# Expert tiles run among the chunks of the recurrence, in an order worked out ahead

## Chip, core and metric

One core of a Trainium2 chip runs the whole program. The metric is the device time of one execution in microseconds. Engines are named as the profile does: PE is TensorE, DVE VectorE, ACT ScalarE, POOL GpSimd, SP the queue that issues plain DMAs.

## What is computed

A gated recurrence over 4 sequences of 5056 tokens with 256 features, and then a layer of 8 experts of which each of the 20224 tokens uses the one with the largest cosine score:

```python
sig = 1.0 / (1.0 + np.exp(-f_logit))
f = lower_bound + (1.0 - lower_bound) * sig
h = f[:, t] * h + (1.0 - f[:, t]) * x[:, t]      # for each t; y[:, t] = h
...
logits = (y / norm(y)) @ (emb / norm(emb)).T / tau
expert_idx = np.argmax(logits, axis=1)
gate_w = softmax(logits) at expert_idx
out[mask] = gate_w[mask, None] * (np.maximum(y[mask] @ w1[e], 0.0) @ w2[e])   # for each expert e
```

w1 is 256 x 1024 and w2 is 1024 x 256 for each expert.

## The kernel before

Every instruction is recorded as an operation with its engine and what it depends on (`Prog.op`). Each engine executes its operations in the order in which they were recorded; `resolve` turns the dependences into semaphore waits. So the program's text sets the order on each of the five queues.

The recurrence goes over 40 chunks of 512 tokens (the last has 256). For a chunk, `load` brings 512 tokens of f_logit and x through SP into one of three input buffers each; `F_` and `X_` turn them on PE, eight f32 transposes each, into two PSUM banks each; `gate_` makes the gate (ACT); `scan_` forms nx and runs the scan of both feature halves (DVE); `yo_` turns the result back, `yev_` copies it to the row buffer `Yt` (ACT), `sq_` squares it (ACT). Two chunks form a group for the router (the last two chunks are groups of their own, 21 groups in all): `lg_` makes logits and squared norms (PE), `rt_` turns them, `d1_` finds the expert, `psl_` counts with small matmuls the place of each token in its expert's rows of a scratch tensor in device memory (XsScratch), `d2_` and `d3_` finish place and weight, and one indirect DMA per 128 tokens on POOL scatters rows of 264 bf16 (256 features, weight, token number) there. The loop over `c` records these stages some chunks apart, and every second chunk one of the 16 weight loads (`wload`, POOL, f32 to bf16).

After the last group the number of tokens per expert is known. Some 20 small DVE instructions make the list of tiles (`tbl`: first row and expert of each of 86 tiles of 256 rows), 16 indirect DMAs fill the rows behind each expert's last token with null rows (L904), and the expert tiles follow: `xload` brings a tile through SP at an address read from the list, `yt_` turns it (four bf16 transposes, DVE copy), `mm1` does 16 w1 matmuls into four banks, ACT and DVE apply the relu, `mm2` does 16 w2 matmuls into two banks, ACT and DVE apply the weight, and two indirect DMAs on POOL write the 256 rows of the output (L1019). Each tile load waits for all scatters:

```python
scat_all = [scat[g] for g in range(NG)]
a_done = [h_tr, h_te, scat_all, h_nt]
...
xsh[j] = op(
    "sp", fn, a_done, hnull if j >= NFULL else None,
    odh[j - NX] if j >= NX else None, dma=f"xs{j % NX}",
)
```

There are six tile buffers (`NX`), two of the turned tile, two of the hidden layer, four of the output (`NO`). The four banks of `mm1`, the two of `mm2` and the two of `yt_` are the eight that the recurrence used.

Of the kernel before, what the change touches and what calls it, by code (L numbers as in the profile page):

```python
# [2 lines left out]

# [3 lines left out]
P = 128  # L7
# [8 lines left out]
class Handle:  # L16
    __slots__ = ("eng", "fn", "deps", "dma", "val", "know", "used")

    def __init__(self, eng, fn, deps, dma):
        self.eng, self.fn, self.deps, self.dma = eng, fn, deps, dma  # L20
        self.val, self.know, self.used = 0, None, False


class Prog:

    def __init__(self):
        self.order = []
        self.dma_count = {}  # L30

    def op(self, eng, fn, *deps, dma=None):
        flat = []

        def add(d):
            if d is None:
                return
            if isinstance(d, (list, tuple)):
                for x in d:
                    add(x)  # L40
            else:
                flat.append(d)

        add(deps)
        h = Handle(eng, fn, flat, dma)
        if dma is not None:
            self.dma_count[dma] = self.dma_count.get(dma, 0) + 16
            h.val = self.dma_count[dma]
        self.order.append(h)
        return h  # L50

    def resolve(self):
        for h in self.order:
            for d in h.deps:
                d.used = True
        count, know, plan = {}, {}, {}
        for h in self.order:
            kn = know.setdefault(h.eng, {})
            waits = {}
            for d in h.deps:  # L60
                key = d.dma if d.dma is not None else d.eng
                if kn.get(key, 0) >= d.val:
                    continue
                waits[key] = max(waits.get(key, 0), d.val)
            for d in h.deps:
# [6 lines left out]
            if h.dma is None and h.used:  # L72
                count[h.eng] = count.get(h.eng, 0) + 1
                h.val = count[h.eng]
            h.know = dict(kn)
            plan.setdefault(h.eng, []).append((h, sorted(waits.items())))
        return plan

    def emit(self, nc, es, block):
# [3 lines left out]
        def sem(key):  # L83
            if key not in sems:
                sems[key] = es.enter_context(nc.semaphore(name=f"s_{key}"))
            return sems[key]

        for eng, items in plan.items():
            for h, waits in items:
                for key, _ in waits:  # L90
                    sem(key)
                if h.dma is not None:
                    sem(h.dma)
                elif h.used:
                    sem(eng)

        def run(eng):
            def body(e):
                for h, waits in plan.get(eng, []):
                    for key, v in waits:  # L100
                        e.wait_ge(sems[key], v)
                    with nc.allow_low_precision(reason="whole numbers below 2**24"):
                        ins = h.fn(e)
                    if h.dma is not None:
                        ins.then_inc(sems[h.dma], 16)
                    elif h.used:
# [11 lines left out]
def bass_hgrn_recurrence__then__cosine_router_kernel(  # L118
# [23 lines left out]
    NFULL = (N - E * (T - 1) + T - 1) // T  # L142
    NT = N // T + E - 1
    NULLROW = E * CAP
    MAGIC = 12582912.0

# [7 lines left out]
    with ExitStack() as es:  # L154
# [6 lines left out]

        ident = sb("ident", [P, P])
# [6 lines left out]
        half = sb("half", [P, 8])  # L169
        scr = sb("scr", [P, P])  # L170
        iop = sb("iop", [P, 1])
        io17 = sb("io17", [P, 17])
        ex17 = sb("ex17", [P, 17])
        base17 = sb("base17", [P, 17])
        nio = sb("nio", [P, E, 2])
# [7 lines left out]
        w1b = sb("w1b", [P, E, DT, Fdim], BF16)  # L183
        w2b = sb("w2b", [P, E, FT, D], BF16)

        xin = [sb(f"xin{q}", [P, 4, D]) for q in range(3)]
        fin = [sb(f"fin{q}", [P, 4, D]) for q in range(3)]
        th = [sb(f"th{q}", [P, DT, CH]) for q in range(2)]
        fg = [sb(f"fg{q}", [P, DT, CH]) for q in range(2)]
        nx = [sb(f"nx{q}", [P, DT, CH]) for q in range(2)]  # L190
        hb = [sb(f"hb{q}", [P, DT, CH]) for q in range(4)]
        sq = [sb(f"sq{q}", [P, DT, CH]) for q in range(3)]
        lgS = [sb(f"lgS{q}", [P, CH]) for q in range(2)]
        NY = 4
# [887 lines left out]
```

## Time and profile before

| | |
|---|---|
| median of 3 runs | 820.59 us (818.81 to 821.49) |
| the profiled execution | 821.09 us, span 819.3 us |
| mean granted TensorE clock | 0.856 of full speed |
| busy in the span: PE, DVE, ACT, POOL | 606.0, 390.4, 332.6, 414.0 us |

The busy times are sums over the span; which engine matters differs by stretch. Granted clock 1.00 is 2.4 GHz, 0.5 is 1.2 GHz; a mean between them says how much of a stretch ran at each.

### The profile page before, as it was taken

What the parts mean: (1) busy time and instruction counts of PE and PEld (TensorE: products, weight loads), DVE (VectorE), ACT (ScalarE), POOL (GpSimd) and SP (SyncE); (2) the same over time, 40 slices, a digit from 0 to 9 for tenths busy, and PEclk for the clock granted to TensorE, in tenths of its full rate; (3) what the DMA queues carried; (4) which work ended last, traced back from release to release, by engine and by line L of the source; (5) the groups of instructions that cost most, each with busy time, mean ns of one, the idle gap of its engine ahead of it and who ended that gap; (6) DMA issues with size and microseconds to landing.
All of it is one profiled execution on the core that took longest, in us unless ns stands there. A gap on an engine that the chain in (4) does not pass through costs nothing.

```text
span 819.3 us, 14640 instructions
## 1 busy us (share of the span) xinstructions
PE 606.0 (74%) x4649; PEld 456.7 (56%) x4649; DVE 390.4 (48%) x817; ACT 332.6 (41%) x503; POOL 414.0 (51%) x466
## 2 busy tenths in 40 slices
PE   3665666665666665656033999999999999999994
PEld 3444455444445444442012777777777777777773
DVE  3555555555444444454121555555555555555552
ACT  4644444445454445452000433333433343344331
POOL 4056655555565564553773444444444444444443
PEclk9977777778777877785555999999999999999998
DMA  9756566766656664400121223333322332323220
GB/s 262 232 154 157 155 155 171 159 163 183 163 175 155 171 159 127 122 26 14 50 69 44 86 86 99 98 99 95 96 93 93 99 99 93 97 89 96 80 61 13
DMA packets 78868, 95.02 MB, mean 116 GB/s; under 512 B 9217, under 2 KB 68877, under 8 KB 78800
## 3 DMA queue, kind: packets, MB, share of 16 engines
q1 hardware_dynamic: 54416, 53.06, 22.3%
q0 software_dynamic: 24384, 41.02, 18.2%
q8 instruction: 46, 0.75, 0.4%
q14 instruction: 22, 0.18, 0.1%
HBM read 69.83 MB, written 34.44 MB: 127 GB/s over the span
## 4 chain that ended last, share of the span: by engine, by line
PE 70%; issue 10%; ACT 7%; DVE 6%; POOL 3%; another core or an unknown queue 2%; DMA 1%; SPq 0%; POOLq 0%; DVEq 0%; ACTq 0%
PE y_ps L994 18%; PE fl_ps L965 12%; PE xT_ps L965 11%; PE xT_ps L492 7%; PE fl_ps L477 6%; PE y_ps L558 6%; PE lg_ps L584 5%; ACT sq L548 3%; ACT Yt L571 3%; POOL XsScratch L777 2%; DVE nx L520 2%; PE lg_ps L940 1%; PE rt_ps L940 1%; PE rt_ps L631 1%
## 5 line engine op out<-in xcount | busy, mean ns | idle before, releaser
L1019 POOL DMA_INDIRECT out_dram<-osb,xsb x172 | 169.5, 986 | 202.6 <-ACT hT L980 152.2
L777 POOL DMA_INDIRECT XsScratch<-Yt,sli x158 | 155.1, 981 | 144.5 <-DVE Yt L759 100.1
L994 PE MATMUL y_ps<-w2b,hT 128*128 x1376 | 165.3, 274 | 0.9 <-DVE osb L1012 0.9
L994 PEld LDWEIGHTS y_ps<-w2b,hT 128*128 128x128 bf16 x1376 | 131.4, 98 | 15.4 <-issue 1.1
L965 PE MATMUL fl_ps<-ys,w1b 128*128 128x256 bf16 x688 | 104.1, 284 | 17.1 <-DVE ys L950 14.9
L571 ACT ACTIVATE Yt<-y_ps 128x1024 bf16<-128x1024 f32 (+1 forms) x40 | 40.5, 1013 | 181.6 <-PE y_ps L558 168.7
L1009 ACT ACTIVATE osb<-y_ps,xsb 128x256 f32<-128x256 f32 x86 | 40.8, 474 | 177.6 <-PE y_ps L994 175.7
L965 PE MATMUL xT_ps<-ys,w1b 128*128 128x256 bf16 x688 | 103.6, 283 | 0.2 <-issue 0.2
L965 PEld LDWEIGHTS fl_ps<-ys,w1b 128*128 x688 | 66.3, 96 | 60.8 <-issue 40.6
L584 PE MATMUL lg_ps<-hb,eT 128*8 128x512 f32 (+1 forms) x160 | 54.8, 784 | 57.6 <-ACT sq L548 57.6
L538 DVE TENSOR_TENSOR_SCAN hb<-fg,hb,nx 128x512 f32<-128x512 f32 (+4 forms) x78 | 93.5, 1238 | 1.4
L985 DVE TENSOR_SCALAR hT<-fl_ps 128x512 bf16<-128x512 f32 x86 | 59.5, 692 | 59.6 <-PE fl_ps L965 56.6
L1012 DVE TENSOR_SCALAR osb<-y_ps,xsb 128x256 f32<-128x256 f32 x86 | 41.6, 484 | 91.1 <-PE y_ps L994 90.1
L644 DVE TENSOR_REDUCE rmax<-rt_ps 128x8 f32<-128x64 f32 (+2 forms) x21 | 4.6, 221 | 167.1 <-issue 92.5
L492 PE MATMUL xT_ps<-ident,xin 128*128 128x128 f32 x316 | 67.0, 381 | 22.8 <-DVE nx L520 16.3
L492 PEld LDWEIGHTS xT_ps<-ident,xin 128*128 128x128 f32 x316 | 53.8, 200 | 50.7 <-issue 32.1
L965 PEld LDWEIGHTS xT_ps<-ys,w1b 128*128 x688 | 66.5, 97 | 25.2 <-issue 1.6
L985 DVE TENSOR_SCALAR hT<-xT_ps 128x512 bf16<-128x512 f32 x86 | 59.5, 692 | 42.8 <-PE xT_ps L965 30.9
L980 ACT ACTIVATE hT<-xT_ps 128x512 bf16<-128x512 f32 x86 | 51.4, 597 | 44.0 <-PE xT_ps L965 38.4
L980 ACT ACTIVATE hT<-fl_ps 128x512 bf16<-128x512 f32 x86 | 51.3, 596 | 28.9 <-PE fl_ps L965 13.3
L510 ACT ACTIVATE fg<-th,cs 128x512 f32<-128x512 f32 (+1 forms) x80 | 60.3, 801 | 1.3
L477 PE MATMUL fl_ps<-ident,fin 128*128 128x128 f32 x316 | 58.5, 347 | 1.1 <-ACT th L504 1.1
(123 smaller groups left out, 685.7 us busy)
## 6 DMA issues: line engine op xcount, KB each, us to landing
fin<-in_f_logit_dram SPq DMA_DIRECT2D x39, 512.0 KB
xin<-in_x_dram SPq DMA_DIRECT2D x39, 512.0 KB
xsb<-XsScratch SPq DMA_DIRECT2D x86, 132.0 KB
w1b<-in_moe_w_dram POOLq DMA_DIRECT2D x8, 512.0 KB, 5.9
w2b<-in_moe_w_dram POOLq DMA_DIRECT2D x8, 512.0 KB, 12.2
out_dram<-osb,xsb POOLq DMA_INDIRECT x172
XsScratch<-Yt,sli POOLq DMA_INDIRECT x158
fin<-in_f_logit_dram SPq DMA_DIRECT2D x1, 256.0 KB
```

The source lines that it names most:

```text
L477: i = e.transpose(fl_ps[:, dh, b * P : (b + 1) * P], fin[q][:, b, dh * P : (dh + 1) * P], ident[:],)
L492: i = e.transpose(xT_ps[:, dh, b * P : (b + 1) * P], xin[q][:, b, dh * P : (dh + 1) * P], ident[:],)
L510: lambda e, dh=dh: e.activation(fg[q][:, dh, 0:n], th[q][:, dh, 0:n], AF.Identity, bias=cs[:, dh, 0:1], scale=cs[:, dh, 1:2],),
L538: lambda e, dh=dh, s0=s0, s1=s1, init=init: e.tensor_tensor_scan(hb[c % 4][:, dh, s0:s1], fg[q][:, dh, s0:s1], nx[q][:, dh, s0:s1], init, ...
L571: lambda e: e.activation(Yt[g % NY][:, k_ * 4 : k_ * 4 + nb, 0:D], y_ps[:, 0:nb, :], AF.Copy),
L584: i = e.matmul(lg_ps[32 * k_ : 32 * k_ + 8, 0:n], eT[:, kt, :], hb[c % 4][:, kt, 0:n], start=(kt == 0), stop=(kt == DT - 1),)
L777: lambda e, j=j, b=b, k_=k_: e.indirect_dma_start(out=Xs[:, :], out_offset=bass.IndirectOffsetOnAxis(ap=sli[g % 4][:, j : j + 1], axis=0), ...
L965: i = e.matmul(ph[g][:, fi * T : (fi + 1) * T], w1b[:, bass.ds(ev, 1), kt, f * P : (f + 1) * P], ys[j % 2][:, kt, :], start=(kt == 0), sto ...
L980: lambda e, g=g, o=o: e.activation(o, ph[g], AF.Relu),
L985: lambda e, g=g, o=o: e.tensor_scalar(o, ph[g], 0.0, None, op0=ALU.max),
L994: i = e.matmul(po[s], hT[j % 2][:, kf, s * P : (s + 1) * P], w2b[:, bass.ds(ev, 1), kf, :], start=(kf == 0), stop=(kf == FT - 1),)
L1019: lambda e, s=s: e.indirect_dma_start(out=out[:, :], out_offset=bass.IndirectOffsetOnAxis(ap=xsb[j % NX][:].bitcast(I32)[:, s, 129:130], a ...
```

## The change

The instructions are no longer executed in the order of the text. Each operation now names what it reads, writes and which PSUM bank it uses, an estimated cost and a priority (`pr.prio`); dependences follow from the names. `schedule` then walks through the program as a small model of five engines and one DMA bus would: at each step the engine that is free first takes the ready operation with the smallest priority. The order that comes out is the order on each queue.

The list of tiles is made in eight steps (`update_`): after groups 5, 7, 9, 11, 13, 15 and 17 the tiles that are certain to be full by then are appended, 17 after the first and 8 after each of the next six, and the last 21 after group 20. A tile depends on the scatters up to its step's group, and only the last 21 wait for the null rows, which eight plain DMAs on SP now write in place of 16 indirect ones on POOL. All tiles still wait for all 16 weight loads; these are recorded one per chunk (chunks 0 to 15). A chunk's operations have the chunk's number as priority; the tiles of a step that follows chunk k have k + 3, k + 3.5, k + 4 and so on.

The first 70 tiles use three banks: 5 for the transposes and two of the four w1 pieces, 6 for the other two, 7 for w2. The recurrence keeps banks 0 to 4: `F_`, `X_` and `Y_` now work in halves of a chunk with one bank each, four transposes and one eviction at a time. The router's gate (`gate_`) is done for two groups at once, so scatters come in batches of 16, and the scaling of the norms moves from POOL to DVE. The list holds the expert's offset in the weights ready for use in place of its number.

```diff
+        for k in x:
+            edge(self.writer.get(("x", k)), True)
+            self.writer[("x", k)] = o
...
+    def schedule(self):
...
+        bus = 0.0
+        out = []
+        while True:
+            best = None
+            for e in free:
+                while wait[e] and wait[e][0][0] <= free[e]:
...
+                break
+            s, e = best
+            if avail[e]:
+                p, i, o = heapq.heappop(avail[e])
...
+                t, p, i, o = heapq.heappop(wait[e])
+            o.start = s
+            free[e] = s + o.cost
+            if o.dma is not None:
+                bus = max(bus, free[e]) + o.nbytes / self.DMA_RATE
+                o.end = max(bus, free[e]) + self.DMA_FIX
+            else:
...
+            out.append(o)
+            for q, hard in succ[id(o)]:
+                t = (o.end + self.LAT) if hard else free[e]
+                if q.eng == e and o.dma is None and hard:
+                    t = o.end + 60
+                ready[id(q)] = max(ready[id(q)], t)
+                left[id(q)] -= 1
+                if left[id(q)] == 0:
...
+        def wload(i, c):
...
+            op(
+                "pool", lambda e: e.dma_start(dst, src), 1000, w=[("w", i)], dma=f"w{i}",
+                r=[("hb", c % NH, 0)], nbytes=1 << 20,
+            )
+
...
+        batches = [[g, g + 1] for g in range(0, NG - 3, 2)] + [[g] for g in range(NG - 3, NG)]
+        bof = {g: (i, bb.index(g)) for i, bb in enumerate(batches) for g in bb}
...
         def F_(c):
...
+            for dh in range(DT):
+                def fn(e, dh=dh):
...
+
...
+                pe(fn, 135 * nb, r=[("fin", q), "ident"], x=[BF])
...
+                )
...
         def X_(c):
...
+
+                pe(fn, 135 * nb, r=[("xin", q), "ident"], x=[BX])
...
-            for dh in range(DT):
+                    n, r=[("fg", c % 2, dh)], w=[("nx", c % 2, dh)], x=[BX],
...
+        def Y_(c):
...
+            pe(
+                lg, 3000, x=[BL],
+                r=["eT", "onesf"] + [("hb", c % NH, d) for c in cc for d in range(2)]
+                + [("sq", c % NSQ) for c in cc],
+            )
...
+        def gate_(bi):
...
+            pool(
+                lambda e: e.tensor_tensor(nr2[q][:, 0:JJ], nrm[q][:, 0:JJ], half[:, 0:JJ], ALU.pow),
+                1900, r=[("nrm", q), "half"], w=[("nr2", q)],
+            )
+            dve(
+                lambda e: e.tensor_scalar(
+                    nr2[q][:, 0:JJ], nr2[q][:, 0:JJ], 1e-6, tau, op0=ALU.add, op1=ALU.mult
+                ),
+                8, r=[("nr2", q)], w=[("nr2", q)],
+            )
...
+                        op(
...
+                            1280, r=[("Yt", y), ("Ytg", y), ("Yti", y), ("ytz", y), ("sli", y)],
+                            w=[("Xs", g)], dma=f"sc{y}", nbytes=67584, chain=False,
+                        )
...
+        def update_(u, g, last):
...
+            pe(
+                lambda e: e.matmul(
+                    bank[BT][:, 456:464], onesb[:], fin_oh[:, 64:72], start=True, stop=True
+                ),
+                100, r=[("oh", (g + 1) % 3), "onesb"], x=[BT],
+            )
...
+            dve(
+                lambda e: e.tensor_tensor(acc[b][:], acc[a][:], dac[:], ALU.add),
+                2, r=["dac0", "dac1", ("acc", a)], w=[("acc", b)],
+            )
+            dve(
+                lambda e: e.tensor_scalar(
+                    tbl[u][:, 0:1], acc[b][:, 0:1], iop[:, 0:1], float(T),
+                    op0=ALU.add, op1=ALU.mult,
+                ),
+                1, r=[("acc", b), "iop"], w=[("tbl", u)],
+            )
+            dve(
+                lambda e: e.tensor_copy(tbl[u][:, 1:2], acc[b][:, 1:2]), 1,
+                r=[("acc", b)], w=[("tbl", u)],
+            )
+            if last:
+                for e_ in range(E):
+                    def nul(e, e_=e_):
...
+                    op(
+                        "sp", nul, 700, r=["nrow", "nulr"], w=["nul"], dma="nu", nbytes=135168,
+                        chain=False,
...
+        def tile_(j, u, g, phb, pob, ysb):
...
+            rd = [("tbl", u), ("nt", 0), ("nt", 1)]
+            rd += [("Xs", g_) for g_ in range(g + 1)]
+            if last:
+                rd += ["nul"]
+            op("sp", ld, 700, r=rd, w=[("xsb", qx)], dma=f"xs{qx}", nbytes=135168)
+
+            ysT = bank[ysb][:, 0:256].bitcast(BF16)
...
+            pr.prio -= YBOOST
+            pe(yt, 310, r=[("xsb", qx), "identb"], x=[ysb])
+            dve(
+                lambda e: e.tensor_copy(ys[qy][:].rearrange("p k c -> p (k c)"), ysT),
+                512, True, x=[ysb], w=[("ys", qy)],
+            )
...
+            for m in range(4):
+                pb = phb[m % len(phb)]
+
+                def mm1(e, m=m, pb=pb):
+                    if m == 0:
+                        evr[j] = e.value_load(
+                            tbl[u][j : j + 1, 1:2], min_val=0, max_val=(E - 1) * WE
+                        )
...
+                                wb[0][:, bass.ds(evr[j] + (kt * Fdim + (2 * m + fi) * P), P)],
...
+                prev = pe(
+                    mm1, 490, r=[("ys", qy), ("tbl", u)] + [("w", i) for i in range(2 * E)],
+                    x=[pb], order=[prev],
+                )
...
+            po = [bank[pob[0]][:, 0:D], bank[pob[1]][:, D : 2 * D]]
+            one = pob[0] == pob[1]
+            for m in range(4):
+                def mm2(e, m=m):
...
+                                wb[1][:, bass.ds(evr[j] + kf * D, D)],
...
+                pe(
+                    mm2, 480, r=[("hT", qh, m)] + [("w", i) for i in range(2 * E)],
+                    x=sorted(set(pob)), order=[prev],
+                )
...
+                    1280, r=[("osb", qo, s), ("xsb", qx)], w=[("out", j, s)], dma=f"od{qo}_{s}",
+                    nbytes=131072,
...
+        last_of = {cc[-1]: g for g, cc in enumerate(groups)}
+        ups = [5, 7, 9, 11, 13, 15, 17] + [NG - 1]
+        avail = []
+        for u, g in enumerate(ups):
+            tok = sum(nof(c) for gg in range(g + 1) for c in groups[gg])
+            k = max(0, -(-(tok - E * (T - 1)) // T)) if u < len(ups) - 1 else NT
+            avail += [(u, g)] * (k - len(avail))
+        MERGED = 70
+        NWC = 16
+        YBOOST = 1.5
+
+        def put(j):
+            u, g = avail[j]
+            pr.prio = groups[g][-1] + 3.0 + 0.5 * (j - avail.index((u, g)))
+            if j < MERGED:
+                tile_(j, u, g, (5, 6), (7, 7), 5)
+            else:
+                tile_(j, u, g, (0, 1, 2, 6), (3, 7), 4)
+
+        for c in range(NCH):
+            pr.prio = c
+            if c >= 2:
+                load(c)
+            F_(c)
+            X_(c)
+            Y_(c)
+            for i in range(2 * E * c // NWC, 2 * E * (c + 1) // NWC):
+                if i < 2 * E:
+                    wload(i, c)
...
+            if c in last_of:
+                g = last_of[c]
+                route_(g)
+                bi, gi = bof[g]
+                if g == batches[bi][-1]:
+                    gate_(bi)
+                if g in ups:
+                    u = ups.index(g)
+                    update_(u, g, g == NG - 1)
+        for j in range(NT):
+            put(j)
+        pr.prio = 1 << 20
+        op("pool", lambda e: e.nop(), 50, deps=[pr.writer[("out", j, s)] for j in range(NT) for s in range(2)],
...
+        pr.total = pr.schedule()
```

## Rows read from the trace of the kernel before

**Rows 1.** Busy us by engine (x count) in stretches of the span, clock, DMA

```profile
core 0: us, PE busy (x) PEld busy (x) DVE busy (x) ACT busy (x) POOL busy (x), PEclk, DMA share, GB/s
100.00:300.00 200.00, 124.62 (x812) 95.11 (x816) 105.11 (x226) 96.99 (x124) 118.76 (x124) 0.76 0.63 163
300.00:340.00 40.00, 24.08 (x152) 17.66 (x144) 19.12 (x40) 18.23 (x24) 19.74 (x22) 0.74 0.51 144
391.00:444.00 53.00, 8.00 (x49) 4.31 (x49) 8.19 (x47) 3.03 (x7) 35.89 (x42) 0.54 0.20 60
444.00:809.00 365.00, 361.37 (x3072) 278.16 (x3072) 186.81 (x340) 140.36 (x256) 166.97 (x170) 0.99 0.28 88
```

**Rows 2.** Chain that ended last, low clock: start us, us, what

```profile
158.34 1.97 PE xT_ps L492 x8
160.31 1.71 PE fl_ps L477 x8
...
181.82 1.72 PE y_ps L558 x8
...
216.19 1.97 PE xT_ps L492 x8
```

**Rows 3.** The same chain at full clock, with a group's router work

```profile
185.58 0.60 PE lg_ps L584
...
187.48 1.03 PE xT_ps L492 x8
188.51 0.87 PE fl_ps L477 x8
...
193.25 0.56 PE rt_ps L631 x4
...
195.16 0.24 PE rt_ps L697
...
195.73 1.13 issue
...
209.23 0.89 PE y_ps L558 x8
```

**Rows 4.** Groups of instructions: busy us, mean ns | idle before, releaser

```profile
L777 POOL DMA_INDIRECT XsScratch<-Yt,sli x158 | 155.1, 981 | 144.5 <-DVE Yt L759 100.1 <-issue 41.8 <-DVE q L848 1.1
L685 POOL TENSOR_SCALAR nr<-nr 128x8 f32<-128x8 f32 (+2 forms) x21 | 15.2, 725 | 1.9
L456 POOL DMA_DIRECT2D w2b<-in_moe_w_dram x8 | 8.0, 995 | 0.4
L730 DVE RECIPROCAL rs<-nr 128x8 f32<-128x8 f32 (+2 forms) x21 | 4.1, 193 | 19.0 <-POOL nr L685 18.9
```

**Rows 5.** Timeline of one expert tile: start us, us, engine, line

```profile
604.51 0.60 ACT L980 ACTIVATE hT<-xT_ps 128x512 bf16<-128x512 f32 x1 [0.43 <-PE xT_ps L965]
...
604.81 0.39 PE L940 MATMUL rt_ps<-identb,xsb 128*128 128x128 bf16 x4
605.03 1.91 PE L994 MATMUL y_ps<-w2b,hT 128*128 x16
...
605.62 0.41 DVE L950 COPY ys<-rt_ps 128x512 bf16<-128x512 bf16 x1
...
607.08 1.15 PE L965 MATMUL fl_ps<-ys,w1b 128*128 128x256 bf16 x8
608.15 1.15 PE L965 MATMUL xT_ps<-ys,w1b 128*128 128x256 bf16 x8
```

**Rows 6.** DMA issues: count, KB each, us from issue to landing

```profile
w2b<-in_moe_w_dram POOLq DMA_DIRECT2D x8, 512.0 KB, 12.2
```

**Rows 7.** PE's timeline: first, last of the recurrence, first tile

```profile
11.00 1.97 PE L477 MATMUL fl_ps<-ident,fin 128*128 128x128 f32 x8
...
391.18 0.64 PE L558 MATMUL y_ps<-ident,hb 128*128 128x128 f32 x4
...
424.90 0.58 PE L940 MATMUL lg_ps<-identb,xsb 128*128 128x128 bf16 x4 [9.78 <-DMA xsb<-XsScratch]
```

More of the change, by code (lines that the diff above doesn't have):

```diff
@@ L13 @@
 AX = mybir.AxisListType
[L16 to L21, printed above, removed]
+class Op:
+    __slots__ = (
+        "eng", "fn", "deps", "order", "dma", "val", "know", "used", "cost", "nbytes", "prio",
+        "idx", "start", "end", "tag",
+    )
 class Prog:
+    LAT = 90
+    DMA_FIX = 1900
+    DMA_RATE = 300.0
@@ L28, in __init__, with op, edge @@
     def __init__(self):
[L29 to L36, printed above, removed]
+        self.ops = []
+        self.writer = {}
+        self.readers = {}
+        self.dma_last = {}
+        self.prio = 0
+    def op(self, eng, fn, cost, r=(), w=(), x=(), deps=(), order=(), dma=None, nbytes=0, prio=None, tag="", chain=True):
+        o = Op()
+        o.eng, o.fn, o.cost, o.dma, o.nbytes = eng, fn, cost, dma, nbytes
+        o.val, o.know, o.used, o.tag = 0, None, False, tag
+        o.prio = self.prio if prio is None else prio
+        o.idx = len(self.ops)
+        need, order = {}, {id(q): q for q in order if q is not None}
+        def edge(q, bank=False):
+            if q is None or q is o:
@@ L37, in add @@
                 return
[L38 to L50 removed]
+            if (
+                q.eng == eng and q.dma is None and dma is None and (eng == "pe" or bank)
+            ):
+                order[id(q)] = q
+            else:
+                need[id(q)] = q
@@ new lines, in flat @@
+        def flat(t):
+            if t is None:
+                return
+            if isinstance(t, (list, tuple)):
+                for y in t:
+                    yield from flat(y)
+            else:
+                yield t
+        for q in flat(deps):
+            need[id(q)] = q
+        for k in r:
+            edge(self.writer.get(k))
+            self.readers.setdefault(k, []).append(o)
+        for k in w:
+            if chain:
+                edge(self.writer.get(k))
+            for q in self.readers.get(k, ()):
+                edge(q)
+            self.writer[k] = o
+            self.readers[k] = []
@@ L71, in resolve @@
                         kn[k] = v
[L72 to L76, printed above, removed]
+            o.know = dict(kn)
+            plan.setdefault(o.eng, []).append((o, sorted(waits.items())))
         return plan
```

1250 lines of the change are left out of this document (583 added, 667 removed).

## Prediction

> **What bounds the kernel now.** I read four views, in this order. First the busy time by stretch [rows 1]. It shows a kernel in three pieces. From 11 us to about 391 us the recurrence and the router run, and in the 200 us sampled there no engine is full: TensorE (PE) 62%, VectorE (DVE) 53%, ScalarE (ACT) 48%, GpSimd (POOL) 59%, at a mean granted clock of 0.76. From 391 to 444 us nearly nothing runs on PE (8.0 us busy in 53). From 444 to 809 us the expert tiles keep PE busy for 361 of 365 us at clock 0.99, while DVE and ACT are busy 51% and 38%. So the first piece is bound by waits between engines whose queues are in order, the second by the last scatters, the tile list and the first loads, the third by PE. Second, the chain of waits in the first piece: the same transposes stand there at both clock levels [rows 2, 3], 1.97, 1.71 and 1.72 us for eight at 1.2 GHz and 1.03, 0.87 and 0.89 at 2.4 GHz. The start of the same step six chunks apart gives the pace: (216.19 - 158.34)/6 = 9.64 us a chunk [rows 2]. Third, the instruction groups [rows 4]: POOL issues 330 indirect DMAs at 0.98 us, plus 0.30 us of issue time between two (41.8 us over 137 gaps), so 1.28 us each. Fourth, PE's timeline in the third piece [rows 5]: the transposes of a tile, its 16 w2 matmuls and 16 w1 matmuls follow without holes; 365/86 = 4.24 us a tile.
>
> **What PE has to do in all.** At 2.4 GHz a chunk costs PE 1.03 + 0.87 + 0.89 for its three transposes, and half a group's router work: logits 187.48 - 185.58 = 1.90, transposes 0.56, prefix matmuls 195.73 - 195.16 = 0.57 [rows 3]. That is 2.79 + 1.52 = 4.30 us, or 170 us for 39.5 chunks. The 86 tiles take 365 us. Together 535 us, against a span of 819.3: 11.0 us of lead-in [rows 7], some 210 us in which the first piece waits or is clocked low, 53 us of hole, 10.3 us of tail (819.3 - 809) [rows 1]. The change can take from the 210 and the 53; it takes no matmul away.
>
> **Part by part.**
> (a) *Weights.* One load per chunk instead of one per two, for chunks 0 to 15; each tile still waits for all 16. The last is issued after the scan of chunk 15 and lands some 12.2 us later [rows 6]. So no expert matmul can start before 16 chunks are through, however early the list is there.
> (b) *Pace until then.* With half a load per chunk the DMA engines are busy 0.63 x 9.64 = 6.1 us a chunk, without 0.51 x 9.64 = 4.9 [rows 1]; with a whole one about 7.3. POOL: 118.8 us in 20.75 chunks is 5.7, plus some 1.4 of issue gaps; half a load more (1.0 + 0.3)/2 = 0.65, the scaling of the norms moved to DVE -0.7/2 = -0.35 [rows 1, 4]: 7.4. PE needs 4.3 to about twice that by its clock, DVE and ACT 5. The halved evictions (tanh, copy to Yt, nx) add instructions on engines that are half idle. So the pace lies between 7.4 and today's 9.64. I take 8.0, nearer to the queue bounds, because four transposes and a half eviction in place of eight and a whole one halve each step that the next engine waits for. 16 x 8.0 = 128 us, and 12 us for the weights, in which PE does 1.5 chunks more.
> (c) *Merged stage.* 22 chunks are left. Priorities are chunk number against 14, 14.5, ... for the tiles; up to the last chunk 59 tiles come before it (17 + 5 x 8 + 2), that is 2.7 per chunk. PE's work: 22 x 4.30 + 59 x 4.24 = 95 + 250 = 345 us, or 15.7 us per chunk. POOL per chunk: 6.1 without weight loads + 2.7 x 2 x 1.28 = 13.0 (83%). DVE: 105.1/20.75 = 5.1, + 2.7 x 186.8/86 = 5.9, + the updates, about 17 small instructions at 0.19 us [rows 4] per four chunks, 0.8: 11.8 (75%). ACT 4.7 + 4.4 (58%). So PE stays the fullest, but POOL is close, and its scatters come in batches of 16 (20.5 us) between which the tiles' output must pass. How much of the stage PE loses to waits no row shows: the third piece loses 1%, the first 38% [rows 1]. With two independent streams to take work from I place it near the former: 12%, 345/0.88 = 392 us; the ends are 349 and 556.
> (d) *PSUM.* The merged tile has banks 5, 6 and 7 only. Bank 5 takes the transposes, two w1 pieces and three evictions: 0.39 + 0.41 + 2 x (0.53 + 0.60) [rows 5], about 3.1 us plus six handovers, under the 5.8 us (15.7/2.7) between tiles. Nothing added.
> (e) *Address arithmetic.* Each w1 matmul still takes one register step, now on a ready product. Today eight take 608.15 - 607.08 = 1.07 us, 134 ns each; the w2 ones, one step per two, about 1.91/16 = 119 [rows 5]. A gain is at most 15 ns x 1376 = 21 us; a loss of the same size isn't excluded. I take 0.
> (f) *End of the recurrence.* The last list waits for the route of chunk 39, its scatters and eight null writes, moved to SP (on POOL they are 16, 16 x 1.28 = 20 us; eight at that price would be 10 us beside the scatters). Today 424.90 - 391.18 = 34 us pass from the last transposes to the first tile [rows 7]. Six tiles (25 us) are left to cover about 30. I take 5 us, between 0 and 17. If nothing were left as cover it would cost 30. All loads of the last 21 tiles queue behind the null writes on SP; chunk loads are through by then.
> (g) *Queues.* SP is passed by 65 tile loads that used to follow the last chunk load. A tile load waits for a free buffer, hence for the output scatter six tiles earlier, and a chunk load behind it waits too. Three input buffers hide two to three chunks of that, 31 to 47 us at 15.7; I cost it at nothing, and rival C prices it.
> (h) *Rest.* 27 tiles at 4.24 = 114 us, tail 10.3.
>
> **Sum**: 11 + 128 + 12 + 392 + 5 + 114 + 10 = 672 us of span; the profiled execution took 821.1 at a span of 819.3, so 674, on a base whose median is 820.6.
>
> **A rule weighed.** The granted clock was 0.99 while PE was 99% busy and 0.76 while it was 62% busy [rows 1]. The Trainium skill, TensorE: Matmul & The Clock Gate, section "A second HAM failure mode: psum-queue depth-cycling", says that matmul groups that cycle through PSUM banks can idle so often for short times that the clock swings between its levels. It speaks against the three banks of (d). No row of this kernel shows it, as the third piece has eight banks in use; rival B is what it would do.
>
> **Rivals.**
> A, *late start*: the weights or the first lists come late behind scatters on POOL, and tiles begin some eight chunks later; the change then does half of what it says. Each such chunk leaves PE 8.0 - 4.30 = 3.7 us idle: +30, 704 us. For it: every tile waits for all weights, and the DMA engines run close to full; against: POOL has slack.
> B, *clock*: the merged stage runs at the 0.76 of the first piece. 345/0.76 = 454 us instead of 392: 736. For it: PE pieces there stay half a microsecond long between waits; against: two streams fill it.
> C, *slower*: the queues lock. Chunk loads stand behind tile loads on SP, these behind output scatters, these behind batches of 16 scatters on POOL, and PE keeps the 62% of today's first piece: 345/0.62 = 556, in all 838. It decides from the point where the merged stage exceeds 392 + 147 = 539 us, a PE share of 64%.
> D, *better*: the first 16 chunks at 7.4 (118 us), 5% lost in the merged stage (363), no hole at the end: 630.
>
> **How the numbers follow.** Forecast 674 with 0.60, A 0.13, B 0.13, C 0.06, D 0.08. The bounds of the unknown costs move the sum by -44 (D) to about +75 (9.64 a chunk is +26, 20% lost instead of 12% is +39, the hole 17 instead of 5 is +12), so I give 625 to 755, which leaves out C, half of D and the far end of B. A measurement here tells 0.3% from no change. Faster 0.93, same 0.01, slower 0.06, all of the last from C.
>
> **What would show it.** Right: first expert matmul at about 150 us; from there to some 540 us both kinds of work in every slice, PE 85 to 90% busy at a clock above 0.95; no hole over 10 us near the last chunk; 4.2 us a tile after it. (b) is wrong if chunk 15 comes before 125 or after 165 us; (c) if PE is under 80% busy between; (f) if PE stands still for over 15 us before the last list; B shows in the clock row, C as chunk loads that wait on SP for output scatters. The prediction fails first with the 12%.

## The result, and the profile after

| | before | changed |
|---|---|---|
| median, same chip | 821.04 us (818.81 to 822.3, 4 runs) | 777.0 us (770.92 to 781.91, 4 runs) |
| ratio, 95% interval | | 0.9463 (0.9382 to 0.9544) |
| profiled execution | 821.09 us, span 819.3 | 781.91 us, span 780.0 |

The sign was forecast, the size was not: 777 lies above the range of 625 to 755. A run over 1.5% above the fastest of its kernel counts as slow and is left out of every time below; there is one, 787.5 us of the experiment e13. The page of the changed kernel, first busy time by engine, then two rows of its 40 slices, then the shares of the chain that ended last:

```profile
PE 591.7 (76%) x4656; PEld 430.5 (55%) x4656; DVE 399.0 (51%) x923; ACT 342.8 (44%) x574; POOL 387.7 (50%) x410
...
PE   5876676658868996879984698289848866999994
...
PEclk9998869769979999999997699579957977999997
...
PE 61%; another core or an unknown queue 11%; DVE 8%; issue 7%; ACT 7%; POOL 4%; DMA 1%; POOLq 0%; ACTq 0%; DVEq 0%
```

From the first expert matmul on (slice 10) PE should stand at 8 or 9. It dips to 4, 6 and 2, and the clock with it. And 11% of the chain, some 85 us, has no releaser that the profile knows. The first expert matmul, in the view of its line (shortest, median and longest ns, first and last start of those in the stretch looked at):

```profile
L1036 PE MATMUL bank<-ys,w1b x8: 272/273/421, 176.6 to 177.7; 128*128 128x256 bf16 x8
```

Two stretches, from there to the last transposes of the last chunk and from these to the last tile; columns as in [rows 1]:

```profile
176.00:634.00 458.00, 354.40 (x2874) 261.82 (x2873) 231.05 (x531) 188.26 (x326) 220.21 (x218) 0.88 0.32 101
634.00:769.00 135.00, 121.94 (x986) 90.77 (x984) 64.39 (x149) 45.55 (x86) 59.47 (x61) 0.96 0.24 75
```

The merged stage takes 458 us, with PE busy 77% of it; forecast were 392 and 88%. The view of waits names what was waited for when an engine stood idle; these groups, 159.3 us in sum with the four left out, end at "remote", that is at no instruction or transfer on record (line, total us, times, longest):

```profile
ACT osb L1081 <- remote: 37.3, 7, 13.6
...
ACT Yt L626 <- remote: 29.2, 5, 6.7
...
DVE hT L1056 <- remote: 20.1, 6, 7.9
...
DVE ys L1021 <- remote: 15.5, 1, 15.5
DVE slt L756 <- remote: 15.4, 3, 6.3
```

The nine groups are all of instructions that read what PE wrote. One such place in the timeline (start, length, engine, line, operation):

```profile
417.73 1.06 PE L618 MATMUL bank<-ident,hb 128*128 128x128 f32 x4
...
419.59 0.69 DVE L1056 TENSOR_SCALAR hT<-bank 128x512 bf16<-128x512 f32 x1 [1.71 <-PE bank L618]
...
421.53 1.05 ACT L611 ACTIVATE sq<-hb 128x1024 f32<-128x1024 f32 x1
...
421.69 0.40 PE L1013 MATMUL bank<-identb,xsb 128*128 128x128 bf16 x4 [2.89 <-ACT hT L1051]
...
422.81 0.91 PE L1067 MATMUL bank<-w2b,hT 128*128 x4
...
425.05 0.96 POOL L832 DMA_INDIRECT XsScratch<-Yt,sli  x1 [0.30 <-issue]
426.31 0.96 POOL L832 DMA_INDIRECT XsScratch<-Yt,sli  x1 [0.30 <-issue]
427.58 0.96 POOL L832 DMA_INDIRECT XsScratch<-Yt,sli  x1 [0.30 <-issue]
428.10 0.60 ACT L626 ACTIVATE Yt<-bank 128x512 bf16<-128x512 f32 x1 [5.52 <-remote]
...
432.67 0.98 POOL L1091 DMA_INDIRECT out_dram<-osb,xsb  x1 [0.30 <-issue]
435.10 0.42 DVE L1021 COPY ys<-bank 128x512 bf16<-128x512 bf16 x1 [14.82 <-issue]
```

PE's transposes L618 end at 418.79; ACT is free from 422.58 and copies them only at 428.10. The tile's transposes L1013 end at 422.09; DVE, idle since 420.28, copies them at 435.10, 13.0 us later. (The view books this second wait to "issue", so the 159.3 us leave it out.) Meanwhile POOL issues one scatter after another. I call this a late hand-over from PE. For a count I took every instruction of DVE and ACT whose last dependence is a PE operation (and that waits for no recent transfer), and the time from that operation's recorded end to its start. With no indirect DMA close by the median is 37 ns. Where PE ended beside the fifth or a later indirect DMA of a row on POOL there are 25 such starts, mean 2.8 us. In all 43 starts are over 0.6 us late, together 131 us.

### The profile page after: what moved, and what is told of

Same layout as the page of the kernel before. It is cut to its first block, busy times and chain, and to the rows that moved or that the text cites. A ratio compares the mean times of both kernels' runs of the same rounds, so it can differ in the third digit from the quotient of the medians.

```text
span 780.0 us, 14923 instructions
## 1 busy us (share of the span) xinstructions
PE 591.7 (76%) x4656; PEld 430.5 (55%) x4656; DVE 399.0 (51%) x923; ACT 342.8 (44%) x574; POOL 387.7 (50%) x410
## 4 chain that ended last, share of the span: by engine, by line
PE 61%; another core or an unknown queue 11%; DVE 8%; issue 7%; ACT 7%; POOL 4%; DMA 1%; POOLq 0%; ACTq 0%; DVEq 0%
PE bank L1036 23%; PE bank L1067 19%; PE bank L618 4%; PE bank L546 4%; PE bank L575 3%; PE bank L666 3%; PE bank L1013 3%; POOL XsScratch L832 3%; DVE hb L599 2%; ACT hT L1051 2%; POOL nr L775 2%; DVE hT L1056 2%; DVE nx L583 1%; ACT th L554 1%
## 5 line engine op out<-in xcount | busy, mean ns | idle before, releaser
L1036 PE MATMUL bank<-ys,w1b 128*128 128x256 bf16 x1376 | 217.1, 290 | 57.3 <-issue 26.5
L1036 PEld LDWEIGHTS bank<-ys,w1b 128*128 x1376 | 135.5, 99 | 130.8 <-issue 92.0
L832 POOL DMA_INDIRECT XsScratch<-Yt,sli x158 | 164.0, 1038 | 82.9 <-issue 45.4
L1067 PE MATMUL bank<-w2b,hT 128*128 x1376 | 186.1, 282 | 21.2 <-DVE hT L1056 20.8
L1056 DVE TENSOR_SCALAR hT<-bank 128x512 bf16<-128x512 f32 x172 | 118.2, 687 | 90.7 <-PE bank L1036 54.7
L1067 PEld LDWEIGHTS bank<-w2b,hT 128*128 128x128 bf16 x1376 | 131.4, 101 | 43.6 <-issue 24.2
L1051 ACT ACTIVATE hT<-bank 128x512 bf16<-128x512 f32 x172 | 102.4, 596 | 114.5 <-PE bank L1036 87.9
L618 PE MATMUL bank<-ident,hb 128*128 128x128 f32 x316 | 57.3, 311 | 33.4 <-issue 15.2
L546 PE MATMUL bank<-ident,fin 128*128 128x128 f32 x316 | 58.0, 314 | 23.8 <-ACT th L554 10.3
L618 PEld LDWEIGHTS bank<-ident,hb 128*128 128x128 f32 x316 | 40.4, 158 | 54.9 <-issue 33.2
L583 DVE SCALAR_TENSOR_TENSOR nx<-fg,bank 128x512 f32<-128x512 f32 (+1 forms) x80 | 53.9, 673 | 31.6 <-PE bank L575 8.5
L575 PE MATMUL bank<-ident,xin 128*128 128x128 f32 x316 | 56.6, 308 | 8.9 <-DVE nx L583 8.0
```

Source lines behind the costliest of these rows:

```text
L546: i = e.transpose(bank[BF][:, b * P : (b + 1) * P], fin[q][:, b, dh * P : (dh + 1) * P], ident[:],)
L575: i = e.transpose(bank[BX][:, b * P : (b + 1) * P], xin[q][:, b, dh * P : (dh + 1) * P], ident[:],)
L583: lambda e, dh=dh: e.scalar_tensor_tensor(out=nx[c % 2][:, dh, 0:n], in0=fg[c % 2][:, dh, 0:n], scalar=1.0, in1=bank[BX][:, 0:n], op0=ALU. ...
L618: i = e.transpose(bank[BY][:, (b % 2) * D + dh * P : (b % 2) * D + (dh + 1) * P], hb[c % NH][:, dh, b * P : (b + 1) * P], ident[:],)
L832: lambda e, j=o + j, i=o + k_ * 4 + b: e.indirect_dma_start(out=Xs[:, :], out_offset=bass.IndirectOffsetOnAxis(ap=sli[y][:, j : j + 1], axis=0
L1036: i = e.matmul(bank[pb][:, fi * T : (fi + 1) * T], wb[0][:, bass.ds(evr[j] + (kt * Fdim + (2 * m + fi) * P), P)], ys[qy][:, kt, :], start= ...
```

## The experiments

Kernels sent together ran on one chip, beside new runs of the kernel before. All times are medians; "unknown" is the sum of the waits that end at "remote" in the profile of that kernel.

| set | before | kernel | time | ratio (95%) | unknown |
|---|---|---|---|---|---|
| first | 821.0 | the change | 777.0 | 0.946 (0.938 to 0.954) | 159.3 |
| 1 | 800.9 | e1 bursts of 8 | 636.4 | 0.795 (0.791 to 0.798) | 0 |
| 1 | | e2 paced scatters | 661.5 | 0.825 (0.822 to 0.829) | 0 |
| 1 | | e3 tiles last | 710.9 | 0.889 (0.885 to 0.892) | 0 |
| 1 | | e4 before, bursts of 16 | 809.0 | 1.010 (1.006 to 1.014) | 0 |
| 2 | 801.0 | e5 the change again | 641.1 | 0.801 (0.800 to 0.803) | 0 |
| 2 | | e6 bursts of 8 again | 636.2 | 0.794 (0.792 to 0.796) | 0 |
| 3 | 831.4 | e7 bursts of 8, weights by chunk 10 | 782.6 | 0.941 (0.938 to 0.944) | 172.2 |
| 3 | | e8 before again | 830.7 | | 52.4 |
| 4 | 831.4 | e9 paced again | 731.6 | 0.879 (0.871 to 0.887) | 47.2 |
| 4 | | e10 the change again | 781.9 | 0.940 (0.935 to 0.944) | 188.5 |
| 5 | 831.1 | e11 longer pauses | 766.6 | 0.923 (0.918 to 0.929) | 55.2 |
| 5 | | e12 tiles last again | 785.7 | 0.945 (0.938 to 0.953) | 163.3 |
| 6 | 834.7 | e13 no data | 774.8 (one run) | | 154.4 |
| 6 | | e14 no issue on POOL | 632.9 | 0.758 (0.754 to 0.763) | 0 |
| 6 | | e15 null tiles | 779.8 | 0.934 (0.931 to 0.937) | 146.0 |

**Set 1: long bursts as the suspect.** e1 lets the scatters go by one group:

```diff
-        batches = [[g, g + 1] for g in range(0, NG - 3, 2)] + [[g] for g in range(NG - 3, NG)]
+        batches = [[g] for g in range(NG)]
```

> The changed kernel with the scatters of one group (8) instead of two (16) let go at a time, as in the kernel before; ten more norm powers on POOL. Theory S (signals): in the trace of the changed kernel an engine that waits for TensorE starts 37 ns (median) after TensorE's recorded end, but 2.4 us later on the mean when TensorE ended beside the 5th to 8th scatter in a row and 5.9 us beside the 9th to 12th; the stops follow from many scatters back to back. It expects most of the late starts gone: handoffs over 1 us down from about 140 us in sum to under 60, time 690 to 735. Theory Q (POOL's queue): output scatters and powers wait behind the bursts and buffers come free late. Halved bursts halve that wait, but ten powers add 25 to 29 us on POOL: 750 to 780, and handoffs between TensorE and its readers as late as before. Theory C (clock): the low granted clock alone makes TensorE slow; nothing here changes it: 770 to 780.

e2 puts POOL work between the scatters of a batch of 16 (`gap` keeps the order):

```diff
+                        gap[0] = pool(lambda e: e.memset(gapb[:], 0.0), 700, order=gap, w=["gapb"])
-                        op(
+                        gap[0] = op(
```

> The changed kernel with one memset of 128x512 on POOL ahead of every recurrence scatter, so that no two of them stand back to back; batches of 16 as they are. Theory S: late starts of TensorE's readers go away or shrink to well under half; POOL does some 158 x 0.7 = 110 us more beside it, so the time falls to 710 to 765. Theory Q: POOL's queue gets longer, everything that waits behind the batches waits longer: 800 to 890. Theory C: no change in the clock, 775 to 800.

e3 puts the tiles behind the recurrence:

```diff
-            pr.prio = groups[g][-1] + 3.0 + 0.5 * (j - avail.index((u, g)))
+            pr.prio = NCH + 3.0 + 0.5 * j
```

> The changed kernel with all tile priorities behind the last chunk, so that the recurrence runs first and the tiles after it; the lists, batches of 16, banks and halved evictions as they are. It prices the interleaving apart from the rest. From the changed kernel's trace chunk 15's scan ends at 122 us, 7.4 us a chunk: 39.5 chunks at 7.4 to 8.0 are 292 to 316 us, with 11 us of lead-in, some 34 us of hole and 86 tiles at 4.24 us and a tail of 10: 712 to 736 if the scatter bursts do in the second half what they do in the first. Theory S: late starts of TensorE's readers stay in the recurrence's bursts and are gone in the tiles. Theory Q expects none without output scatters in the way, and a recurrence at the 7.4 us that POOL's work allows: 700 to 712. Theory C: TensorE half idle, clock low as in the kernel before, 9 us a chunk: 770.

e4 edits the kernel before: the scatter loop becomes `scatters(g)`, called at every second group for two.

```diff
+            held.append(g)
+            if g % 2 or g >= NG - 3:
+                while held:
+                    scatters(held.pop(0))
```

> The kernel before with one edit: the 8 scatters of every even group are held and issued together with the 8 of the next group, 16 in a row; not one instruction more or less. Theory S: late starts of TensorE's readers appear in the first piece, where the kernel before has almost none (three over 1 us); nine bursts with some 5 to 10 us of stop each: 850 to 910. Theories Q and C: in the first piece no output scatter waits behind the bursts, POOL has the same work, and three more buffers cover the later landing: 815 to 830.

e1 came out far below what its theory gave, and e2 with it, although e2 kept the batches of 16. No profile of this set has a late hand-over at all (no start is over 0.4 us late), not in e3, where up to 26 scatters stand in a row, and not in e4, whose bursts of 16 cost 1%. So no edit of this set had removed the cause: it was not there. The kernel before was 20 us quicker too.

**Set 2: the change itself, again.**

> The changed kernel itself, word for word, beside fresh runs of the kernel before. In the four runs so far no engine started late after TensorE in any profile (37 ns median at every place in a burst, up to 26 scatters in a row), and the kernel before took 801 us there against 821 beside the first runs of the changed kernel. Two readings. Kernel: batches of 16 together with interleaved tiles are what makes TensorE's signals late; then they are late here too, some 110 to 150 us in sum, and the time is 750 to 780. Run: the late signals belong to the chip or the time of those first runs, and no edit took them away; then there are none here and the time is 630 to 660, since the paced batches of 16 took 661 with 110 us more work on POOL and the bursts of 8 took 636.

> The bursts of 8 once more, beside the changed kernel on the same chip. Kernel reading: 630 to 645 again, 110 to 150 us less than the changed kernel. Run reading: within 15 us of the changed kernel, to either side: half as long a wait behind a burst, against ten more powers of some 2.5 us on POOL.

The reading "run" holds: the same kernel takes 641 us here, and bursts of 8 are worth 5 us (their intervals don't meet), not 140. Its page (busy row, clock row, chain):

```profile
PE 553.7 (87%) x4656; PEld 407.9 (64%) x4656; DVE 397.0 (62%) x923; ACT 342.5 (54%) x574; POOL 394.3 (62%) x410
...
PEclk9999797967999999999999999999998999999997
...
PE 63%; POOL 5%; DVE 4%; ACT 3%; issue 3%; DMA 1%; SPq 0%; POOLq 0%; DVEq 0%; ACTq 0%
```

The first expert matmul, the same two stretches, and the same two copies in the timeline:

```profile
L1036 PE MATMUL bank<-ys,w1b x69: 272/280/281, 157.4 to 178.0; 128*128 128x256 bf16 x69
```

```profile
157.00:500.00 343.00, 326.09 (x2868) 247.06 (x2869) 229.30 (x531) 187.68 (x325) 229.38 (x217) 1.00 0.44 136
500.00:625.00 125.00, 118.64 (x989) 89.12 (x986) 64.80 (x149) 46.26 (x86) 63.56 (x65) 1.00 0.28 86
```

```profile
352.87 0.60 PE L618 MATMUL bank<-ident,hb 128*128 128x128 f32 x4
353.10 0.96 POOL L832 DMA_INDIRECT XsScratch<-Yt,sli  x1 [0.30 <-issue]
...
353.12 1.05 ACT L611 ACTIVATE sq<-hb 128x1024 f32<-128x1024 f32 x1
...
353.30 0.39 PE L1013 MATMUL bank<-identb,xsb 128*128 128x128 bf16 x4
...
353.73 0.42 DVE L1021 COPY ys<-bank 128x512 bf16<-128x512 bf16 x1 [0.41 <-PE bank L1013]
...
354.07 0.59 ACT L626 ACTIVATE Yt<-bank 128x512 bf16<-128x512 f32 x1
```

The transposes of the same chunk end at 353.47, within a burst as long, and ACT copies them at 354.07, late only by the square it was busy with. The unknown share of the chain is gone; the merged stage takes 343 us with PE busy 95% at full clock. Beside the fifth or a later indirect DMA in a row 174 starts now come 48 ns after PE on the mean. Issue times are the same (L832: 1.04 us each in the first profile, 1.05 here).

**Set 3: bursts of 8 with earlier weights, and the kernel before.**

> Bursts of 8, and the 16 weight loads spread over the first 10 chunks instead of 16, to price the step that no tile starts before all weights are there. In the bursts-of-8 trace the scan of chunk 15 ends at 117 us, the last weight load is issued at 123 and the first expert matmul runs at 159; the DMA engines are busy 80 to 98% until about 120. Weights are the gate: the first expert matmul comes at about 125 to 140 us, and as TensorE is about half idle until then, the time falls by 8 to 15 us, to 621 to 628. The DMA engines are the gate: the chunks come later by what the weights take earlier, the first expert matmul at 145 to 160, time 633 to 642. If this run falls where the late signals are (the kernel before at about 820 instead of 801), bursts of 8 either keep clear of them, with a time within 10 us of these, or do not, with 720 or more.

> The kernel before itself, for its trace where it takes 801 us instead of 821. Run reading: the late starts after TensorE that its first trace has between 429 and 441 us (4.1 and 10.9 us) and at 307 (1.6) are gone, no start later than 0.6 us, and the span is some 17 to 20 us shorter. If the kernel alone made them they are there again, and the 20 us lie elsewhere, spread over the first piece.

```diff
-        NWC = 16
+        NWC = 10
```

Here the kernel before takes 831 us, and late hand-overs are back, with bursts of 8 as well: these don't keep clear of them. In e7 the first expert matmul came at 147 us against 159 in e1, but what early weights are worth can't be read under 172 us of late hand-overs. In the kernel before they are fewer, but there (its waits):

```profile
ACT Yt L571 <- remote: 33.1, 6, 5.6
...
DVE hT L985 <- remote: 13.4, 1, 13.4
...
ACT hT L980 <- remote: 5.9, 1, 5.9
```

Its first profile has 18.1 us of them in three groups, 11.9 at DVE's L985 beside the 16 null scatters. So what differs between the sets is not in the kernel. Sets 1 and 2, on two chips, have hand-overs on time and 801 us for the kernel before; set 3, sets 4 and 5 (one chip) and set 6, on three more, have them late and 831 to 835, and the first pair, with 821, belongs to these. I put it down to the chip, but this is not shown: no chip was measured both ways, and sets 1 and 2 ran one after the other, so the time of the runs could be behind it as well.

**Set 4: pauses between scatters, on a chip with late hand-overs.**

> The paced kernel once more (a memset of 128x512 on POOL ahead of each recurrence scatter), for a place where TensorE's signals come late; the kernel before's own time tells which it is (801 us without late signals, 821 to 831 with them). Without them: 655 to 667 again. With them, if scatters back to back on POOL are what makes them late: late starts stay under 1 us and the time is under 700, less than the changed kernel beside it. If the number of scatters in the air or the tiles beside them make them late, however they are spaced: 750 to 820, no better than the changed kernel.

> The changed kernel, word for word, beside the paced one. Where the kernel before takes about 801 us: 637 to 645, no start over 0.6 us after TensorE's end. Where it takes 820 or more: 765 to 790, with 100 us or more of late starts, all beside scatters.

Some 86 us of extra memsets (158 at 0.54) make the kernel 50 us faster than the change beside it; on time, in set 1, it took 20 us more than the change in set 2. The unknown waits fall from 188.5 to 47.2 us. The starts over 0.6 us late fall less, from 126 us in sum to 80, and single ones are still up to 8.5 us late. The time is between the two forecasts: pauses between the scatters help, but one of 0.54 us doesn't clear the late hand-overs.

**Set 5: a longer pause, and tiles last.** e11 is e2 with a memset of 128x960.

> A longer pause between recurrence scatters: a memset of 128x960 (about 1.0 us) ahead of each instead of 128x512 (0.54 us). POOL gets some 70 us more than in the paced kernel, so where TensorE's signals are on time (the kernel before near 801 us) the time rises, to 690 to 720. Where they come late (820 or more): if it is scatters close behind each other that make them late, the late starts (23 over 1.2 us in the first paced trace of that sort, 114 us of handoffs in sum) fall to a few, and the time comes within 10 us of the 690 to 720; if spacing only spreads them, they stay at over 70 us in sum and the time is 730 to 770.

> All tiles behind the recurrence once more (711 us where the kernel before took 801, with signals on time). Where the signals are late: its recurrence has 158 scatters in batches of 16 and no tile output between them, its tiles have two scatters each 4.3 us. Late signals are a matter of scatters close together: 30 to 70 us in the recurrence, none among the tiles, 740 to 785 in all, no slower than the interleaved kernel (782), so that interleaving gains nothing there. Late signals are a matter of tiles beside scatters: 711 to 725.

e11 settles little: the unknown waits stay at 55 us, the starts over 0.6 us late fall to 45 us in sum, and the longer pauses cost time themselves: POOL, busy 355 of the 470 us from 170 to 640, makes 22% of the chain that ended last, against 4% in the first profile. It does show that a busy POOL alone doesn't make hand-overs late, as with more work on POOL there are fewer of them. e12 says more, though its 785.7 us are just above the 740 to 785 forecast for late signals. Its stretches (recurrence, its end, tiles; same columns), with those of e3 below:

```profile
12.00:334.00 322.00, 220.73 (x1643) 150.12 (x1643) 202.50 (x528) 200.33 (x313) 195.93 (x186) 0.83 0.68 180
334.00:400.00 66.00, 29.85 (x203) 20.40 (x204) 18.24 (x76) 10.59 (x22) 34.48 (x36) 0.71 0.17 54
400.00:770.00 370.00, 345.37 (x2791) 255.21 (x2790) 174.06 (x310) 127.90 (x231) 151.66 (x156) 0.98 0.26 82
```

```profile
12.00:296.00 284.00, 208.64 (x1647) 141.65 (x1647) 201.89 (x533) 199.57 (x315) 199.10 (x185) 0.89 0.76 204
296.00:330.00 34.00, 25.05 (x202) 17.93 (x201) 17.96 (x73) 9.22 (x19) 26.73 (x29) 0.94 0.26 81
330.00:698.00 368.00, 342.32 (x2788) 254.32 (x2788) 173.10 (x309) 128.67 (x233) 160.59 (x166) 0.98 0.27 84
```

The last transposes of the recurrence end at 339.2 us in e12, 5 us behind the first of these cuts, and at 296.0 in e3. So late hand-overs cost the recurrence 43 us and the time from there to the tiles 27 (61 against 34); the tiles, with two scatters every 4.3 us, lose 2. Late hand-overs need no tiles beside the scatters. On such a chip interleaving gains nothing (781.9 against 785.7, intervals overlap); on the others it gains 70 us (641 against 711, across two chips with the same time before).

**Set 6: POOL's issuing or the data.** All three let every tile read the null rows, so that its output rows are dropped: the table's row becomes a constant.

```diff
-                    tbl[u][:, 0:1], acc[b][:, 0:1], iop[:, 0:1], float(T),
-                    op0=ALU.add, op1=ALU.mult,
+                    tbl[u][:, 0:1], acc[b][:, 0:1], 0.0, float(NULLROW),
+                    op0=ALU.mult, op1=ALU.add,
```

e13 adds `bounds_check=0, oob_is_err=False` to the recurrence's scatters; e14 replaces them:

```diff
-                            "pool",
-                            lambda e, j=o + j, i=o + k_ * 4 + b: e.indirect_dma_start(
...
+                            "sp",
+                            lambda e, t=t, i=o + k_ * 4 + b: e.dma_start(
+                                Xs[t % 8 * CAP + 4096 + t // 8 * P :][0:P, :],
+                                Yt[y][:].bitcast(I32)[:, i, :],
+                            ),
```

> The changed kernel with the data of the recurrence scatters left out: each of the 158 indirect DMAs is issued on POOL as before, but with a bound on the row of 0, so that its rows are dropped; and every tile reads the null rows, so that its own output rows are dropped as well (matmuls, loads and issues all stay). Where signals are late (the kernel before at 820 or more): if POOL's issuing of indirect DMAs makes them late, 100 us or more of late starts stay and the time is 740 to 790; if the scattered data on its way makes them late, none stay: 620 to 660. Where they are on time: 620 to 645.

> The other half: the 158 recurrence scatters are replaced by plain DMAs of the same blocks on SP's queue, in token order to rows that nothing reads, so that the same bytes go out and POOL issues none of them; the tiles read the null rows as in the run beside. Where signals are late: if POOL's issuing makes them late, the late starts fall to those beside tile outputs, under 40 us in sum, 625 to 680; if the data makes them late, 100 us or more stay and the time is 740 to 790. Where they are on time: 625 to 650.

> The base of the two runs beside it: the recurrence scatters as they are, with their data, and only the tiles read the null rows, so that the output rows are dropped. Where signals are late: as the changed kernel, 760 to 790, if the tiles' output data has no part in it; under 720 if it has. Where they are on time: 630 to 645.

The software queue's row of e15, e13 and e14 (packets, MB, share), each with the chain of the same kernel:

```profile
q0 software_dynamic: 23872, 19.31, 11.9%
...
PE 62%; DVE 11%; another core or an unknown queue 10%; issue 9%; ACT 6%; POOL 1%; DMA 1%; DVEq 0%; POOLq 0%; ACTq 0%
```

```profile
q0 software_dynamic: 23872, 8.72, 8.4%
...
PE 61%; another core or an unknown queue 11%; DVE 10%; issue 7%; ACT 6%; POOL 4%; DMA 1%; DVEq 0%; POOLq 0%; ACTq 0%
```

```profile
q0 software_dynamic: 18816, 8.62, 10.2%
...
PE 72%; DVE 9%; ACT 6%; issue 5%; POOL 4%; DMA 2%; SPq 2%; POOLq 0%; DVEq 0%; ACTq 0%
```

Dropping the scattered bytes (19.31 to 8.72 MB) leaves the late hand-overs as they are (154.4 us unknown against 146.0) and the time nearly so, 774.8 against 779.8. Taking the 158 scatters off POOL, with all their bytes still sent by SP, takes 147 us: 633, on a chip where the kernel before takes 835; no start is over 0.8 us late. So the scatters that POOL issues make the hand-overs late, not their data. Not all of the 147 us need be late hand-overs, as POOL is also rid of the scatters' own time; no run prices that part on time. Whether it is POOL's instruction or its packets on the software queue, these runs don't part: in e13 the packets stay, nearly empty.

## Why the prediction was wrong

| step | forecast | first profile | e5, hand-overs on time |
|---|---|---|---|
| (a), (b) until the first expert matmul | 151 | 176.6 | 157.4 |
| (c) to the last chunk's last transposes | 392 | 457 | 343 |
| (f), (h) to the last tile | 119 | 135 | 125 |
| tail | 10 | 11 | 11 |
| span | 672 | 780.0 | 635.7 |

The step that failed is the 12% of (c), as the text said it would first; but by a cause that no rival named. It was taken from "the third piece loses 1%, the first 38%" [rows 1], as if waits were a matter of how much work the queues hold. PE lost 23% of the merged stage (354 busy of 458), and with the clock at 0.88 its work took longer besides (354 against 326 in e5). Of the 144 us between the two profiles of this one kernel this stage has 115; 19 lie before it and 10 behind. With POOL's scatters gone (e14) a chip with late hand-overs gives 633 us too. On time, 641 us is in the range, and rival D (630) the nearest, with its 5% lost in the stage and no hole; that is in part luck, as (a) and (b) below were off in opposite directions.

- (a): wrong in both. The last weight load is issued at 128.5 us in e5, 14 us after the scan of chunk 15, as POOL has scatters before it; in e14, without them, the first expert matmul comes at 138.8, 19 us earlier. That is rival A's late start, but not by the weights alone: loads land 8.7 us after issue in e5 (median of the w2 ones), and the first expert matmul comes only 29 us after the last, when PE has been idle for just 0.4 us, behind work of the recurrence in its queue. The stage ends at 498 us in e14 and at 500 in e5, so as far as two chips can be compared the later start costs little.
- (b): the pace I took was too slow. 284 us for 39.5 chunks in e3 are 7.2 us a chunk, under my lower bound of 7.4: POOL is busy 199 of the 284 us, 5.0 a chunk, and some of its scatters wait until later. So at the first expert matmul of e5 20 chunks are through, where I had 17.5, and the merged stage has less work (326, not 345); the 59 tiles in it are as forecast. With late hand-overs the pace is 327/39.5 = 8.3.
- (d): nothing added while both streams run (95%), but alone the three banks cost: in e5 nine tiles after the last chunk take 4.87 us each (507.3 to 551.1, the last list's work among them), the last twelve, on more banks, 4.32.
- (e): right; 4.32 us against 4.24 (365/86, [rows 1]) is a loss of 0.08, where 15 ns on each of 16 matmuls would be 0.24.
- (f): no hole in e5: PE is busy 118.6 of the 125 us. The null writes on SP and the six tiles covered the last list, and no wait of PE there is over 0.9 us, nearer to 0 than to 5. In the first profile PE stands idle for 13 of 135 us.
- (g), rival C: PE waits 5.3 us in all for chunk loads in the changed kernel. The queues don't lock.
- Rival B and its rule: with three banks the granted clock is 1.00 from 157 to 500 us in e5. The Trainium skill's warning (TensorE: Matmul & The Clock Gate, "A second HAM failure mode: psum-queue depth-cycling") doesn't describe this stage. Where the clock does fall it follows the stops: in the first profile it is granted at 1.00 (2.4 GHz) from 412 to 416 us, when PE is busy 1.93 of the 4 us, and at 0.58, mostly 1.2 GHz, over the next 21, when it is busy 7.57.

What could have been read beforehand: the chain of before has 2% with an unknown releaser, and its waits 11.9 us at one instruction, while the null scatters ran (429.6 to 441.5 us). I had counted these into the 53 us between the first piece and the third. A wait without a releaser deserved a rival of its own: what else stands beside it, and how much more of that does the change bring together?

## What to carry to other kernels

Read the waits that end at no known releaser, and what runs beside them; here they were the largest term of the change, and the busy rows show only their consequence. Before a difference is put down to an edit, run the unedited kernel beside the edited ones: e1 alone would have "shown" 140 us for an edit that is worth 5. Indirect DMAs that POOL issues in long rows deserve suspicion where engines wait for PE: three of five chips had late hand-overs beside them, and on one of these the kernel took 147 us more with 158 of them than with POOL rid of them (780 against 633). Pauses between them helped on such a chip (e9, 732 against 782); rows of 8 in place of 16, with earlier weights, did not come out better (e7, 783). No kernel here is best on both sorts of chip: bursts of 8 are on the one (636), paced scatters on the other (732).

## What the runs showed of the hardware

- Beside scatters that POOL issues close together, what PE has done reaches ACT and DVE up to 13 us late in the first profile (37 ns otherwise), in some sets of runs only; what ACT has done reaches DVE in 33 ns and PE in 55 in the same profile (medians; 141 at most). Why sets differ, and why only PE, stays open.
- It is the signal that is late, not its reader. The trace records when a semaphore is raised (not every time: 1012 of PE's 1079 in the first profile). There the semaphore that PE raises goes up at 428.08 us, 9.3 us after the L618 before it and 20 ns before ACT's copy starts; in e5 it goes up 10 ns after the same transposes. The signals come one by one meanwhile, and once the row of scatters is over (433.7) six come within 0.3 us (436.51 to 436.80); the next one (438.98) is 20 ns behind its matmuls.
- Whether the results are late as well, the trace can't tell. The Trainium skill (Perfetto Trace Analysis, "Tensor Engine Instruction (MATMUL, LD_WEIGHTS)") says why: the end that is recorded for TensorE is an estimate, and the signal goes out only after PSUM has acknowledged the write. The trace agrees so far that the recorded ends here precede the starts they release by up to 13.0 us.
- PE goes on starting matmuls meanwhile (421.69 to 423.7 in the timeline above) as long as its own waits are met, so a busy PE is no sign that its results have arrived.
